# Two chained matmul layers after linear attention: the second stage walks its tokens tile by tile, with x blocks and sums kept in SBUF and weights streamed; the first stage gets its own PSUM pool

## The chip, the cores and the metric

The kernel runs on one core of one Trainium2 chip. The metric is the device time of one execution in microseconds (us). Every time below is of the kernel before the change, from its timed runs or from one profiled execution.

## The reference

```python
kv = einsum('bhsd,bhse->bhde', k, v)          # 8 batches, 8 heads, 576 positions, head_dim 64
o = einsum('bhsd,bhde->bhse', q, kv)
x = o / sqrt(mean(o*o) + 1e-6) * g_norm       # then 4608 tokens x 512
h = x @ w_in;  x = (relu(h)**2) @ w_out       # layer 0: 512 -> 2048 -> 512
h = x @ w_in2; return (h*cos(h)) @ w_out2     # layer 1: 512 -> 2048 -> 512
```

All data is float32; the weights come as float64 and are turned to float32 on the chip.

## The kernel before

Every matmul operand is split into a high part and the rest (names that end in h and l), and a product is three matmuls: high by high, high by low, low by high. This keeps nearly float32 accuracy.

**Stage one** makes the attention output x and, in 72 chunks (9 tiles of 512 tokens by 8 of the 16 groups of 128 hidden columns), the plain product of half of layer 0: `layer_in` (L362) multiplies x by w_in, `act_relu2` squares, `layer_out` (L397) multiplies by w_out and adds up in four accumulators, which `evict` writes to DRAM as `p_d`. x itself goes to DRAM as `x_d`. Beside it the weights of the rest are converted: `conv_w` loads 512 KB of raw words, makes float32 of them on VectorE and ScalarE, and writes the result to DRAM as `wi_d` and `wo_d`.

**Stage two** does the other half of layer 0 (m=0) and all of layer 1 (m=1). The tokens are cut into tiles of 1024 (the fifth has 512), the hidden columns into groups q of 512: two groups for m=0, four for m=1. One tile with one group is a slot; there are 30. A slot's first product uses a scheme with seven block products instead of eight: `x_block` makes seven combinations of the four quadrants of x (each 128 partitions x 1024 numbers, or 512 in a half tile), `first_product` (L480, 12 matmuls each, 84 in a slot) multiplies them by seven combined weight blocks `wi`, into the PSUM tiles FA and FB in turn; `keep`, `add` and `last` take the sums out. Then relu squared, or a chain of seven steps for x*cos(x), gives g, split into gh and gl. The second product (L589, 96 matmuls in a full slot) multiplies g by `wo` into the PSUM tiles SA and SB, and `drain` adds the result to a partial sum.

The order of slots is the order of the loops: group outside, tile inside. So the five tiles pass once for each group, in six rounds, and

```python
slots = [(m, t, q) for m in range(2) for q in groups_of[m] for t in range(len(TILES))]
```

makes slots 0 to 4 the first round, 5 to 9 the second and so on. A round loads its weights once (`if t == 0`). The x blocks are made in the first round of a layer, written to DRAM as `xb_d`, and loaded again for each slot of the layer's other rounds. The partial sums go through DRAM as well: `load_ev` loads 128 x 512 numbers ahead of each unit of 12 matmuls, `drain` (L601 for m=0, L606 for m=1) adds on VectorE and stores.

All loads and stores named here are issued by SyncE (SP), in one order, each when its own waits are over. Jobs have a place in time (`at(pos(slot), ...)`), and the 84 and 96 matmuls of a slot are mixed at a fixed rate. From this the framework makes each engine's order. A PSUM tile of the kernel before holds two banks (`psum[n]` of shape 128 x 2 x 512), in stage one too, where `at_bank` gives each use half of such a tile. While stage two runs, until slot 9, the 16 weight pieces of layer 1 are converted (`pairs_in(1, ...)`).

Of the kernel before, what the change touches and what calls it, by code (L numbers as in the profile page):

```python
# [22 lines left out]
def kernel(  # L23
# [42 lines left out]
    ps_p = ctx.enter_context(tc.tile_pool(name="ps", bufs=1, space=PSUM))  # L66
# [10 lines left out]
    y_d = [dram.tile([P, NKC, 2 * ht], F32, name=f"y_d{t0}") for t0, ht in TILES]  # L77
    o_d = [dram.tile([P, NKC, 2 * ht], F32, name=f"o_d{t0}") for t0, ht in TILES]
    xb_d = {
        (m, t, i): dram.tile([P, 2, 2, ht], F32, name=f"xb_d{m}_{t}_{i}")  # L80
        for m in range(2)
        for t, (t0, ht) in enumerate(TILES)
        for i in range(NPR)
    }
# [11 lines left out]
    psum = {n: ps_p.tile([P, 2, 512], F32, name=n) for n in ("FA", "FB", "SA", "SB")}  # L96
    at_bank = {
        "l0": ("FA", 0), "l1": ("FA", 1), "o": ("FB", 0), "ss": ("FB", 1),
        "acc0": ("SA", 0), "acc1": ("SA", 1), "acc2": ("SB", 0), "acc3": ("SB", 1),
    }  # L100
    banks = {"o": ["o", "acc0", "acc2"], "ss": ["ss", "acc1", "acc3"], "l": ["l0", "l1"]}

    def bank_of(tag):
        n, j = at_bank[tag]
        return psum[n][:, j, :]

    def bank(use):
        tag = banks[use].pop(0)
        banks[use].append(tag)
        return bank_of(tag)  # L110
# [3 lines left out]

    pools = {}
# [274 lines left out]
    def layer_out(t, f):  # L390
        wh, wl = (x[:, 1, :] for x in wts[0, f])
        gh, gl = gs.pop((t, f))
        for i in range(NKC):
            o = bank_of(f"acc{i}")
# [13 lines left out]
    xb, wi, wo, kept, hs, ys, evs2, quads = {}, {}, {}, {}, {}, {}, {}, {}  # L408
# [4 lines left out]
    def load_quads(m, t):  # L413
        t0, ht = TILES[t]
        for a in range(2):
            for s in range(2):
                quads[m, t, a, s] = raw = big("x", F32, "xraw", ht)
                if m == 0:
                    for b, s0, done, n in pieces(t0 + s * ht, ht, S):
                        nc.sync.dma_start(  # L420
                            out=raw[:, :, done:done + n], in_=x_d[b][:, 2 * a:2 * a + 2, s0:s0 + n]
                        )
                else:
                    nc.sync.dma_start(out=raw, in_=y_d[t][:, 2 * a:2 * a + 2, s * ht:(s + 1) * ht])

    def x_block(k, i):
        m, t, q = slots[k]
        ht = TILES[t][1]
        h, l = xb[k, i] = [big("x", F32R, f"x{n}", ht) for n in "hl"]
        if q:  # L430
            for a, x in enumerate((h, l)):
                nc.sync.dma_start(out=as32(x), in_=xb_d[m, t, i][:, a])
            return
        b11, b12, b21, b22 = (quads[m, t, a, s] for a in range(2) for s in range(2))

        def combine(x, y):
            new = big("x", F32, "xt", ht)
            nc.vector.tensor_tensor(out=new, in0=x, in1=y, op=ALU.subtract)
            return new

        if i == 3:
            quads[m, t, "t1"] = combine(b12, b11)
            quads[m, t, "t2"] = combine(b22, quads[m, t, "t1"])
# [3 lines left out]
            2: lambda: quads[m, t, "t1"],  # L447
            3: lambda: quads[m, t, "t2"],
            4: lambda: b22,
            5: lambda: combine(b22, b12),  # L450
            6: lambda: combine(b21, quads[m, t, "t2"]),
# [6 lines left out]
    def load_wi(m, q, i):  # L458
        wi[m, q, i] = w = w_p.tile([P, 2, 2, 2, P], F32R, tag="w", name="wi")
        nc.sync.dma_start(out=as32(w[:]), in_=wi_d[m, q][:, W_OF[i]])  # L460

    def load_wo(m, q, c):
        wo[m, q, c] = w = w_p.tile([P, 2, DM], F32R, tag="w", name="wo")
# [6 lines left out]
    def first_product(k, i):  # L470
        m, t, q = slots[k]
        ps = f_bank(k, i)
        w, x = wi[m, q, i], xb[k, i]
# [76 lines left out]

    def units(k):
# [4 lines left out]
    def load_ev(k, j, i):  # L556
        m, t, q = slots[k]
        t0, ht = TILES[t]
        evs2[k, j, i] = e = temp([P, 512], F32, "ev")
        if m:  # L560
            r = j * (ht // P) + i
            if q:
                nc.sync.dma_start(out=e, in_=o_d[t].rearrange("p c n -> p (c n)")[:, r * DM:(r + 1) * DM])
        elif q:
            nc.sync.dma_start(out=e[:, :ht], in_=y_d[t][:, i, j * ht:(j + 1) * ht])
        else:
            for b, s0, done, n in pieces(t0 + j * ht, ht, TOK):
                nc.sync.dma_start(out=e[:, done:done + n], in_=p_d[b][:, i, s0:s0 + n])

    s_count = [0]  # L570

    def second_unit(k, j, i):
        m, t, q = slots[k]
        ht = TILES[t][1]
        ps = bank_of(f"acc{s_count[0] % 4}")
        s_count[0] += 1
        if m == 0:
            ps = ps[:, :ht]
        cs = slice(i * P, (i + 1) * P)
        n = 0  # L580
        for pp in range(2):
            for u in range(2):
                w, g = wo[m, q, 2 * pp + u], gs[k, (u, j)]
                for a, b in ((0, 0), (0, 1), (1, 0)):
                    if m == 0:
                        lhs, rhs = w[:, a, cs], g[b][:, pp, :]
                    else:
                        lhs, rhs = g[b][:, pp, cs], w[:, a, :]
                    nc.tensor.matmul(ps, lhs, rhs, start=(n == 0), stop=(n == 11), skip_group_check=True)  # L589
                    n += 1  # L590
                    if n == 12:
                        drain(k, j, i, ps)
                    yield

    def drain(k, j, i, ps):
        m, t, q = slots[k]
        t0, ht = TILES[t]
        e = evs2.pop((k, j, i))
        if m == 0:
            e = e[:, :ht]  # L600
            nc.vector.tensor_tensor(out=e, in0=ps, in1=e, op=ALU.add)  # L601
            nc.sync.dma_start(out=y_d[t][:, i, j * ht:(j + 1) * ht], in_=e)
            return
        r = j * (ht // P) + i
        if q:
            nc.vector.tensor_tensor(out=e, in0=ps, in1=e, op=ALU.add)  # L606
        elif i % 2:
            nc.scalar.copy(out=e, in_=ps)
        else:
            nc.vector.tensor_copy(out=e, in_=ps)  # L610
        if q == groups_of[1][-1]:
            nc.sync.dma_start(out=out[t0 + r * P:t0 + (r + 1) * P, :], in_=e)
        else:
            nc.sync.dma_start(out=o_d[t].rearrange("p c n -> p (c n)")[:, r * DM:(r + 1) * DM], in_=e)
# [5 lines left out]
    LAG2 = 1.18  # L620
# [223 lines left out]
```

## Time and profile before

| | |
|---|---|
| three timed runs | 1767.85, 1768.12, 1775.46 us |
| the profiled execution | 1766.62 us, span 1764.8 us |
| granted TensorE clock, mean of the span | 0.984 of full speed |
| TensorE matmul busy | 1666.6 us (94%), 7928 matmuls |
| VectorE (DVE), ScalarE (ACT) busy | 1085.8 us (62%), 943.2 us (53%) |
| moved by DMA | 479.63 MB, 272 GB/s over the span |

The span runs from the first to the last instruction; the profiled time is 1.8 us more. Busy time of matmuls overlaps from one to the next, so a stretch can be slow at a high busy share: the number of matmuls in a stretch says more.

### The profile page before, as it was taken

Reading aid. Unit: us, or ns where it says so; the run is one execution under the profiler, and the core shown is the slowest. Engines: PE = TensorE matmul, PEld = TensorE weight load, DVE = VectorE, ACT = ScalarE, POOL = GpSimd, SP = SyncE. Lnnn points to the kernel's source line nnn. Section 1 sums busy time; section 2 is a strip of 40 time slices with the busy share of each in tenths; the row PEclk is TensorE's granted clock in tenths of the full one; section 3 lists DMA queues with packets and bytes.
Section 4 is the critical chain, followed back from the end, with each engine's and each line's share of the span. In section 5 each row is a group of like instructions: output and inputs, shape, how many; then the busy total and the mean of one; then the engine's idle time right before and its main releaser. Section 6 shows DMA issues by size and latency. Waiting matters only on the chain.

```text
span 1764.8 us, 22062 instructions
## 1 busy us (share of the span) xinstructions
PE 1666.6 (94%) x7928; PEld 1318.5 (75%) x7928; DVE 1085.8 (62%) x1522; ACT 943.2 (53%) x1348; POOL 82.0 (5%) x74
## 2 busy tenths in 40 slices
PE   5899999999999998688889999999999999999998
PEld 3677677767787876566667787888888788887887
DVE  6765777776765676544454677855556555556554
ACT  4766776774435555333343656756445555445542
POOL 0101212221000000000000000000000000000000
PEclk9999999999999998988999999999999999999999
DMA  7555777655478989989998997899988999799863
GB/s 273 187 169 159 249 228 229 181 169 167 140 257 318 351 321 316 288 292 321 297 319 288 379 335 299 318 311 327 321 291 277 336 323 312 251 339 326 297 204 101
DMA packets 252492, 479.63 MB, mean 272 GB/s; under 512 B 23520, under 2 KB 124384, under 8 KB 252384
## 3 DMA queue, kind: packets, MB, share of 16 engines
q1 hardware_dynamic: 251616, 475.88, 79.4%
q0 software_dynamic: 768, 2.36, 0.3%
q8 instruction: 62, 1.02, 0.2%
q14 instruction: 46, 0.38, 0.1%
HBM read 301.99 MB, written 176.16 MB: 271 GB/s over the span
## 4 chain that ended last, share of the span: by engine, by line
PE 71%; DVE 9%; DMA 8%; ACT 7%; issue 3%; SPq 1%; POOL 0%; DVEq 0%; ACTq 0%; POOLq 0%
PE SA L589 14%; PE SB L589 14%; PE FA L480 12%; PE FB L480 11%; PE FA L362 8%; PE SA L397 4%; PE SB L397 4%; PE FB L362 2%; DMA xl<-xb_d 1%; DMA wi_d<-raw 1%; DMA xraw<-x_d 1%; DMA xh<-xb_d 1%; DMA ev<-p_d 1%; PE FB L241 1%; DVE h L504 1%
## 5 line engine op out<-in xcount | busy, mean ns | idle before, releaser
L480 PE MATMUL FB<-xh,wi 128*128 128x512 f32 (+1 forms) x840 | 289.7, 376 | 18.4 <-DMA xh<-xb_d 13.6
L480 PE MATMUL FA<-xh,wi 128*128 128x512 f32 (+1 forms) x840 | 285.5, 372 | 8.0 <-DMA xh<-xb_d 6.2
L589 PE MATMUL SB<-wo,gh 128*128 128x512 f32 x576 | 210.9, 397 | 1.1 <-DVE ev L606 1.1
L589 PE MATMUL SA<-wo,gh 128*128 128x512 f32 x576 | 208.6, 394 | 0.6 <-ACT gh L545 0.6
L480 PEld LDWEIGHTS FB<-xh,wi 128*128 128x128 f32 x840 | 159.6, 192 | 50.8 <-DMA xh<-xb_d 11.2
L480 PEld LDWEIGHTS FA<-xh,wi 128*128 128x128 f32 x840 | 156.9, 189 | 40.1 <-DMA xh<-xb_d 5.9
L521 ACT ACTIVATE y<-h,zerob 128x1024 int32<-128x1024 f32 (+1 forms) x80 | 85.2, 1065 | 173.0 <-DVE h L500 172.5
L480 PE MATMUL FB<-xl,wi 128*128 128x512 f32 (+1 forms) x420 | 158.1, 376 | 4.0 <-DMA xl<-xb_d 3.9
L480 PE MATMUL FA<-xl,wi 128*128 128x512 f32 (+1 forms) x420 | 156.2, 372 | 5.2 <-DMA xl<-xb_d 5.2
L589 PEld LDWEIGHTS SB<-wo,gh 128*128 128x128 f32 x576 | 107.5, 188 | 30.9 <-DVE ev L606 7.7
L589 PEld LDWEIGHTS SA<-wo,gh 128*128 128x128 f32 x576 | 107.5, 188 | 28.4 <-DVE ev L606 3.8
L539 DVE SCALAR_TENSOR_TENSOR y<-y,h 128x1024 f32<-128x1024 f32 (+1 forms) x80 | 89.2, 1115 | 53.4 <-ACT y L535 53.2
L525 DVE SCALAR_TENSOR_TENSOR y<-y,h 128x1024 f32<-128x1024 int32 (+1 forms) x80 | 89.4, 1117 | 53.1 <-ACT y L521 52.2
L589 PE MATMUL SA<-gh,wo 128*128 128x512 f32 (+1 forms) x320 | 109.1, 390 | 10.3 <-DVE ev L601 7.2
L589 PE MATMUL SB<-gh,wo 128*128 128x512 f32 (+1 forms) x320 | 107.3, 382 | 11.6 <-DVE ev L601 11.6
L589 PE MATMUL SA<-wo,gl 128*128 128x512 f32 x288 | 112.8, 392 | 0.2 <-DVE gl L549 0.2
L589 PE MATMUL SB<-wo,gl 128*128 128x512 f32 x288 | 112.7, 391 | 0.0
L549 DVE TENSOR_TENSOR gl<-y,gh 128x1024 fp32r<-128x1024 f32 (+1 forms) x80 | 89.1, 1114 | 33.0 <-ACT gh L545 33.0
L362 PE MATMUL FA<-xh,wh 128*128 128x512 f32 x240 | 98.1, 409 | 5.9 <-ACT xh L331 3.7
L531 ACT ACTIVATE y<-y 128x1024 f32<-128x1024 f32 (+1 forms) x80 | 78.0, 975 | 47.7 <-DVE y L525 47.4
L362 PE MATMUL FA<-xl,wh 128*128 128x512 f32 x240 | 96.0, 400 | 0.1
L362 PE MATMUL FA<-xh,wl 128*128 128x512 f32 x240 | 95.7, 399 | 0.0
(162 smaller groups left out, 3301.0 us busy)
## 6 DMA issues: line engine op xcount, KB each, us to landing
xh<-xb_d SPq DMA_DIRECT2D x112, 512.0 KB, 6.9
xl<-xb_d SPq DMA_DIRECT2D x112, 512.0 KB, 7.1
xb_d<-xh SPq DMA_DIRECT2D x56, 512.0 KB, 5.8
xb_d<-xl SPq DMA_DIRECT2D x56, 512.0 KB, 5.6
o_d<-ev SPq DMA_DIRECT2D x108, 256.0 KB, 4.6
ev<-o_d SPq DMA_DIRECT2D x108, 256.0 KB, 5.0
wi<-wi_d SPq DMA_DIRECT2D x42, 512.0 KB, 6.4
kvld<-in_kv SPq DMA_DIRECT2D x32, 512.0 KB, 7.0
```

What stands on the lines that cost most here:

```text
L241: nc.tensor.matmul(kv_ps[b][r, p, r], t[:n, 0, head], t[:n, 1, head], start=(c == 0 and p == 0), stop=(c == NSC - 1), skip_group_check=True,)
L362: nc.tensor.matmul(ps, a[:, 0, cs], m[:], start=(c == 0 and k == 0), stop=(c == NKC - 1 and k == 2))
L397: nc.tensor.matmul(o, a[:, cs], m[:], start=(f == 0 and n == 0), stop=(f == NH - 1 and n == 2), skip_group_check=True)
L480: nc.tensor.matmul(ps[:, pp, :], a, b, start=(i in (0, 1, 2) and n == 0), stop=(n == 5), skip_group_check=True)
L504: nc.vector.tensor_tensor(out=h, in0=f_bank(k, i), in1=t, op=ALU.add)
L521: nc.scalar.activation(out=y.bitcast(I32), in_=hs[k, b], func=AF.Identity, bias=zerob)
L525: nc.vector.scalar_tensor_tensor(out=y, in0=y.bitcast(I32), scalar=-1.0, in1=hs[k, b], op0=ALU.mult, op1=ALU.add)
L531: nc.scalar.activation(out=y, in_=y, func=AF.Sin, scale=math.pi)
L539: nc.vector.scalar_tensor_tensor(out=y, in0=y, scalar=-2.0 * math.pi, in1=hs.pop((k, b)), op0=ALU.add, op1=ALU.mult)
L549: nc.vector.tensor_tensor(out=l, in0=ys.pop((k, b)), in1=as32(h), op=ALU.subtract)
L589: nc.tensor.matmul(ps, lhs, rhs, start=(n == 0), stop=(n == 11), skip_group_check=True)
```

## The change

- The slots go tile by tile: `(m, t, q)` with q inside. A tile's x blocks are made once and stay in SBUF for its two or four slots; nothing is written to or read from `xb_d`.
- The weights `wi` (seven loads of 512 KB) and `wo` (four) are loaded for every slot.
- The partial sums stay in SBUF: four tiles of 128 x 1024 for a tile's life (`sums`), filled from `p_d` for m=0, stored once at the last group.
- The second product takes four units at a time: it goes through the four `wo` pieces outside and the four units inside, so that four accumulators (two in SA, two in SB) are open together, and `drain` takes two of them in one VectorE instruction of 128 x 1024.
- Stage one has a PSUM pool of its own with eight tiles of one bank; the pool of FA, FB, SA, SB opens after it. A pad of 24 numbers per partition ahead of the stage-one tiles becomes 56.
- The jobs get other places: x quadrants 3.6 products ahead, `wi` 2.7, the conversions of layer 1 from slot 0.5 to 8.4 (before 2.5 to 9.2).

```diff
-    psum = {n: ps_p.tile([P, 2, 512], F32, name=n) for n in ("FA", "FB", "SA", "SB")}
+    pools = {}
+    psum = {}
+    def bank_tile(tag):
+        return pools["ps"].tile([P, 512], F32, tag=tag, name=tag)
...
-    slots = [(m, t, q) for m in range(2) for q in groups_of[m] for t in range(len(TILES))]
+    slots = [(m, t, q) for m in range(2) for t in range(len(TILES)) for q in groups_of[m]]
...
     def x_block(k, i):
...
-        h, l = xb[k, i] = [big("x", F32R, f"x{n}", ht) for n in "hl"]
-        if q:
-            for a, x in enumerate((h, l)):
-                nc.sync.dma_start(out=as32(x), in_=xb_d[m, t, i][:, a])
-            return
...
+        l = src.bitcast(F32R) if i in (0, 4) else big("c" if i == 6 else "x", F32R, "xl", ht)
+        xb[m, t, i] = h, l
         nc.scalar.copy(out=h, in_=src)
         nc.vector.tensor_tensor(out=l, in0=src, in1=as32(h), op=ALU.subtract)
-        for a, x in enumerate((h, l)):
-            nc.sync.dma_start(out=xb_d[m, t, i][:, a], in_=as32(x))
...
+    CHUNKS = (1, 3, 0, 2)
+    def sum_tile(k, n):
+        m, t, q = slots[k]
+        j, i = units(k)[2 * n]
+        t0, ht = TILES[t]
+        if q == 0:
+            sums[m, t, n] = e = w_p.tile([P, 2, 512], F32, tag="w", name="sum")
+            if m == 0:
+                for b, s0, done, size in pieces(t0 + j * ht, ht, TOK):
+                    nc.sync.dma_start(out=e[:, :, done:done + size], in_=p_d[b][:, i:i + 2, s0:s0 + size])
+    def second(k, n):
+        m, t, q = slots[k]
+        ht = TILES[t][1]
+        todo = units(k)[4 * n:4 * n + 4]
+        for a, c in enumerate(CHUNKS):
+            pp, u = divmod(c, 2)
+            w = wo[k, c]
+            for b, (j, i) in enumerate(todo):
+                ps = psum["SA" if b < 2 else "SB"][:, b % 2, :512 if m else ht]
+                g = gs[k, (u, j)]
...
+                    last = a == 3 and (x, y) == (1, 0)
+                    nc.tensor.matmul(
+                        ps, lhs, rhs, start=(a == 0 and (x, y) == (0, 0)), stop=last, skip_group_check=True
+                    )
+                    if last and b % 2:
+                        drain(k, 2 * n + b // 2)
+                    yield
     def drain(k, n):
...
+        if q or m == 0:
+            nc.vector.tensor_tensor(out=e, in0=ps, in1=e, op=ALU.add)
         else:
+            nc.scalar.copy(out=e, in_=ps)
+        if q < groups_of[m][-1]:
+            return
...
-    LAG2 = 1.18
+    LAG2 = 1.12
...
-        (pairs_in(1, range(2 * NP)), pos(2.5), pos(9.2)),
+        (pairs_in(1, range(2 * NP)), pos(0.5), pos(8.4)),
...
+            at(pos(k + (f - 2.7) * PH) if k or f > 2 else nA0 - 5 + f / 2, load_wi, k, i)
+        for a, c in enumerate(CHUNKS):
+            at(pos(k + LAG2 - 0.4 + a / 8), load_wo, k, c)
...
-        right("pad", 1).tile([P, 24], F32, name="pad")
+        right("pad", 1).tile([P, 56], F32, name="pad")
...
-    pools["c"] = ctx.enter_context(tc.tile_pool(name="c", bufs=16, side="left"))
-    pools["t"] = ctx.enter_context(tc.tile_pool(name="t", bufs=8, side="left"))
+    ps_p = ctx.enter_context(tc.tile_pool(name="ps", bufs=1, space=PSUM))
+    psum.update({n: ps_p.tile([P, 2, 512], F32, name=n) for n in ("FA", "FB", "SA", "SB")})
+    pools["c"] = ctx.enter_context(tc.tile_pool(name="c", bufs=18, side="left"))
+    pools["t"] = ctx.enter_context(tc.tile_pool(name="t", bufs=4, side="left"))
```

How the instructions stand on two engines shows what moved. On SP before, in the second round (xh and xl are x blocks, ev a partial sum, wh and raw two parts of a converted weight, raw<-in_wB the load of the next one's words):

```order
L432 DMA xl<-xb_d_1_4_112 128x1024
L565 DMA ev<-y_d_91 128x512
L147 DMA raw<-in_wB 128x2x256 x2
L602 DMA y_d_91<-ev 128x512
L432 DMA xh<-xb_d_1_6_114 128x1024
L432 DMA xl<-xb_d_1_6_114 128x1024
L565 DMA ev<-y_d_91 128x512
L602 DMA y_d_91<-ev 128x512
```

On SP now, in a slot of m=0 at the change of a tile:

```order
L451 DMA wo<-wo_d_8_99 128x1024
L446 DMA wi<-wi_d_1_94 128x1024
L134 DMA raw<-in_wB 128x2x256 x2
L451 DMA wo<-wo_d_10_101 128x1024
L553 DMA sum<-p_d_86 128x1024
L446 DMA wi<-wi_d_1_94 128x1024 x2
L594 DMA y_d_90<-sum 128x1024
L161 DMA wi_d_3_98<-wh 896x1x128
L161 DMA wi_d_3_98<-raw 896x1x128
```

Weights stand where the x blocks stood, the loads and stores of partial sums are fewer and larger, and the conversions' loads and stores are still between them.

On TensorE before, where one unit of the second product ends in SA and the next starts in SA's other bank (a new unit begins with wo_11831):

```order
L589 MATMUL SA_203<-wo_11854,gh_12220 128x512
L480 MATMUL FB_202<-xl_12287,wi_11600 128x512
L480 MATMUL FB_202<-xh_12286,wi_11600 128x512 x2
L480 MATMUL FB_202<-xl_12287,wi_11600 128x512
L589 MATMUL SA_203<-wo_11831,gh_12009 128x512
L589 MATMUL SA_203<-wo_11831,gl_12010 128x512
```

On TensorE now, where the last matmul into SA (the first row) ends a group of four units and the next group starts in SA (wo_11423); four rows of SB and three of FB lie in the cut:

```order
L572 MATMUL SA_5631<-wo_11530,gh_11522 128x512
L467 MATMUL FA_5629<-xl_10745,wi_11512 128x512
L572 MATMUL SB_5632<-wo_11530,gh_11522 128x512
L467 MATMUL FA_5629<-xh_10744,wi_11512 128x512
...
L467 MATMUL FB_5630<-xh_10783,wi_11554 128x512
L572 MATMUL SB_5632<-wo_11530,gh_11522 128x512
L467 MATMUL FB_5630<-xl_10785,wi_11554 128x512
L572 MATMUL SA_5631<-wo_11423,gh_11563 128x512
```

Before, the next matmul into the same PSUM tile is the fifth after the last one of the unit; now it is the 14th at this place, and the 13th or 14th at the others.

## Rows read from the trace of the kernel before

**Rows 1.** Windows of the whole core: length, busy us (count) by engine, granted clock, DMA.

```profile
core 0: us, PE busy (x) PEld busy (x) DVE busy (x) ACT busy (x) POOL busy (x), PEclk, DMA share, GB/s
0.00:544.70 544.70, 510.23 (x2714) 378.59 (x2715) 374.60 (x681) 327.48 (x681) 82.02 (x74) 1.00 0.63 204
544.70:749.80 205.10, 182.72 (x811) 148.11 (x809) 134.52 (x175) 106.41 (x119) 0.00 (x0) 0.96 0.91 319
749.80:983.80 234.00, 204.89 (x889) 162.53 (x890) 109.30 (x176) 86.71 (x94) 0.00 (x0) 0.94 0.91 309
983.80:1180.60 196.80, 190.33 (x897) 157.46 (x896) 147.33 (x151) 130.25 (x147) 0.00 (x0) 0.98 0.88 323
1180.60:1368.10 187.50, 187.34 (x854) 153.35 (x852) 103.10 (x108) 97.44 (x104) 0.00 (x0) 1.00 0.90 306
...
1743.10:1764.80 21.70, 16.32 (x68) 12.07 (x66) 6.73 (x10) 3.71 (x6) 0.00 (x0) 1.00 0.21 80
```

**Rows 2.** The same stretches, L589 (second product) alone.

```profile
544.70:749.80 205.10, 114.31 (x384) 72.94 (x384) 0.96 0.91 319
749.80:983.80 234.00, 125.20 (x468) 86.68 (x468) 0.94 0.91 309
983.80:1180.60 196.80, 132.58 (x475) 85.29 (x475) 0.98 0.88 323
1180.60:1368.10 187.50, 143.85 (x433) 79.35 (x432) 1.00 0.90 306
```

**Rows 3.** The chain that ended last, 690 to 1000 us: start, length, what.

```profile
714.33 6.23 DMA ev<-p_d
...
744.09 6.90 DMA xl<-xb_d
...
767.09 4.21 DMA wi_d<-raw
774.37 7.70 DMA xl<-xb_d
```

**Rows 4.** Waits: engine, line, releaser; us in total, times, longest us.

```profile
DVE ev L601 <- DMA ev<-p_d: 25.1, 6, 13.6
...
PE FB L480 <- DMA xh<-xb_d: 13.6, 6, 8.9
...
PEld SB L589 <- DVE ev L606: 7.7, 21, 1.2
...
PE FA L362 <- ACT og L283: 2.1, 4, 0.8
...
PE FB L299 <- ACT og L283: 1.0, 2, 0.7
```

**Rows 5.** DMA issues: what, count, KB each, median us from issue to landing.

```profile
xh<-xb_d SPq DMA_DIRECT2D x112, 512.0 KB, 6.9
...
xb_d<-xh SPq DMA_DIRECT2D x56, 512.0 KB, 5.8
...
o_d<-ev SPq DMA_DIRECT2D x108, 256.0 KB, 4.6
...
wi<-wi_d SPq DMA_DIRECT2D x42, 512.0 KB, 6.4
...
wo<-wo_d SPq DMA_DIRECT2D x24, 512.0 KB, 7.0
...
raw<-in_wB SPq DMA_DIRECT2D x32, 256.0 KB, 4.1
```

**Rows 6.** Groups of VectorE by shape: count, busy us, mean ns, idle before.

```profile
L606 DVE TENSOR_TENSOR ev<-SB,ev 128x512 f32<-128x512 f32 x54 | 37.3, 690 | 82.0 <-PE SB L589 72.6 <-DMA out<-ev 4.7 <-DMA ev<-o_d 3.5
...
L504 DVE TENSOR_TENSOR h<-FB,m 128x1024 f32<-128x1024 f32 x8 | 9.8, 1224 | 12.7 <-PE FB L480 12.3 <-ACT m L494 0.4
```

**Rows 7.** Timeline at 1405 us: the end of a unit and its drain.

```profile
1405.54 0.39 PE L589 MATMUL SB<-wo,gh 128*128 128x512 f32 x1
...
1405.97 0.69 DVE L606 TENSOR_TENSOR ev<-SB,ev 128x512 f32<-128x512 f32 x1 [0.22 <-PE SB L589]
```

**Rows 8.** The chain that ended last: twelve matmuls in a row in either stage.

```profile
479.03 2.78 PE FA L362 x12
...
1347.49 2.73 PE SA L589 x12
```

More of the change, by code (lines that the diff above doesn't have):

```diff
@@ L76 @@
     p_d = [dram.tile([P, NKC, TOK], F32, name=f"p_d{t}") for t in range(NTILE)]
[L77 to L84, printed above, removed]
+    y_d = [dram.tile([P, 2, NKC, ht], F32, name=f"y_d{t0}") for t0, ht in TILES]
     first_pair = (NP, 0)
@@ L407, with load_quads @@
     BLOCKS = {(0, 0): 2, (1, 1): 5, (0, 1): 6, (1, 0): 7}
-    xb, wi, wo, kept, hs, ys, evs2, quads = {}, {}, {}, {}, {}, {}, {}, {}
+    xb, wi, wo, kept, hs, ys, sums, quads = {}, {}, {}, {}, {}, {}, {}, {}
     def big(pool, dtype, name, ht):
         return pools[pool].tile([P, 2, 512], dtype, tag=pool, name=name)[:, :, :ht]
-    def load_quads(m, t):
+    def load_quads(m, t, a):
         t0, ht = TILES[t]
[L415 to L424, printed above, removed]
+        for s in range(2):
+            quads[m, t, a, s] = raw = big("x", F32, "xraw", ht)
+            if m == 0:
+                for b, s0, done, n in pieces(t0 + s * ht, ht, S):
+                    nc.sync.dma_start(
+                        out=raw[:, :, done:done + n], in_=x_d[b][:, 2 * a:2 * a + 2, s0:s0 + n]
+                    )
+            else:
+                nc.sync.dma_start(out=raw, in_=y_d[t][:, s, 2 * a:2 * a + 2, :])
     def x_block(k, i):
@@ L557, in load_ev, with drain @@
+    def drain(k, n):
         m, t, q = slots[k]
         t0, ht = TILES[t]
[L559 to L565, printed above, removed]
-        else:
-            for b, s0, done, n in pieces(t0 + j * ht, ht, TOK):
-                nc.sync.dma_start(out=e[:, done:done + n], in_=p_d[b][:, i, s0:s0 + n])
@@ L570 @@
[L570 to L576, printed above, removed]
-        if m == 0:
[L578 to L608, printed above, removed]
-        else:
[L610 to L614, printed above, removed]
+        j, i = units(k)[2 * n]
@@ new lines, in drain @@
+        ps = psum[("SA", "SB")[n % 2]]
+        e = sums[m, t, n]
+        if m == 0:
+            e, ps = e[:, :, :ht], ps[:, :, :ht]
+        if q or m == 0:
+            nc.vector.tensor_tensor(out=e, in0=ps, in1=e, op=ALU.add)
+        else:
+            nc.scalar.copy(out=e, in_=ps)
+        if q < groups_of[m][-1]:
+            return
+        if m == 0:
+            nc.sync.dma_start(out=y_d[t][:, j, i:i + 2, :], in_=e)
+        else:
+            r = t0 + j * ht + i * P
+            nc.sync.dma_start(out=out[r:r + 2 * P, :].rearrange("(a p) d -> p a d", p=P), in_=e)
@@ L712 @@
                 at(pos(k + (f + 0.25 * (a + 1)) * PH), fn, k, b)
-        todo = units(k)
-        for n, u in enumerate(todo):
-            at(pos(k + LAG2 + (n - 1.5) / len(todo)), load_ev, k, *u)
+        for n in range(len(units(k)) // 2):
+            at(pos(k + LAG2 - 0.2 + 2 * n / len(units(k))), sum_tile, k, n)
     jobs.sort(key=lambda j: j[:2])
@@ L742, in run_slots @@
         seconds = [
-            (k + LAG2 + (n + a / 12) / len(units(k)), k, u, a)
+            (k + LAG2 + n / len(units(k)) / 12, k, n)
             for k in range(len(slots))
-            for n, u in enumerate(units(k))
-            for a in range(12)
+            for n in range(12 * len(units(k)))
         ]
@@ L749, in run_slots @@
         steps1 = (x for k, i in firsts for x in first_product(k, i))
-        steps2 = (x for s0, k, u, a in seconds if a == 0 for x in second_unit(k, *u))
+        steps2 = (x for s0, k, n in seconds if n % 48 == 0 for x in second(k, n // 48))
         nf, ns = 12 * len(firsts), 0
```

71 lines of the change are left out of this document (36 added, 35 removed).

## The prediction

> **What bounds the kernel now.** I read the windows first, cut where the first product of slots 0, 5, 10, 15 and 20 begins, so that each window is one round of five slots [rows 1]. What is to be seen is the number of matmuls beside the length. Stage one ends at 544.7 us and is nearly all TensorE: 510.2 us busy. The fourth round is what stage two can be: 187.5 us, 187.3 of them busy, clock 1.00. The second round has 889 matmuls, only 35 more, and takes 234.0 us at a clock of 0.94. The first takes 205.1 us for 811.
>
> To compare rounds I make the matmuls equal. Each round has 420 of the first product, 84 of them on the half tile's 256 columns; I count those as half (an estimate: by columns), which leaves 378. The second product adds 433 in the fourth round [rows 2], all of 512 columns, as layer 1 moves the weights: 811 in 187.5 us, 0.231 us each. In rounds two and three 96 of the second product's matmuls are half ones (the half slot of m=0): 378 + 468 - 48 = 798 and 378 + 475 - 48 = 805; round one has 378 + 384 = 762. At 0.231 us they should take 184.5, 186.1 and 176.2 us. They took 234.0, 196.8 and 205.1. So 49.5 + 10.7 + 28.9 = 89 us are lost in rounds one to three, and the fourth is the pace without that loss, at a DMA share of 0.90, hardly below the 0.91 of the slow rounds. The share of the transfers alone is therefore not the reason; what counts is who waits for them.
>
> The chain of waits through the slow stretch goes from transfer to transfer: a partial sum (6.2 us), an x block (6.9), a weight store (4.2), an x block (7.7) [rows 3]. In the table of waits TensorE waits for x blocks, 13.6 us in six waits up to 8.9, and VectorE stands at its drain for partial sums, 25.1 us in six waits up to 13.6 [rows 4]; while it stands, what is queued behind it, the adds that free FA and FB, stands too. Both transfers exist only because x blocks and sums live in DRAM.
>
> **The change part by part.** *Removed.* Of full tiles, 112 loads each of xh and xl and 56 stores each at 512 KB (0.524 MB) are 176 MB, and the sums 108 stores and about as many loads of o_d at 0.262 MB, 57 MB [rows 5]; with the half tiles and y_d (not shown) some 274 MB by my count. *Added.* wi goes from 42 loads to 210, wo from 24 to 120 (seven and four for each of 30 slots): 264 more of 0.524 MB, 138 MB. The total falls from 480 to about 344 MB. A slot of m=0 then moves 5.8 MB of weights, half of three transfers of 2.1 MB (x, p_d, y_d), and two conversions of 1.4 MB: 11.8 MB in 41 us, 288 GB/s. That is less than the 306 GB/s of round four, which costs TensorE nothing [rows 1].
>
> What matters more is the lead. In the list of instructions of the program before, the ten closest loads of xh stand 1 to 14 matmuls ahead of their first use, at most 3.2 us, where one takes 6.9 us to land [rows 5]. In the changed list every wi load stands at least 57 matmuls ahead of its use (13 us) and every wo load 77; they take 6.4 and 7.0 us. The cover is thus twice the price; if it is gone, a product waits for the rest of its load. I take the 89 us as gained, with 40 as the lower end (below, second rival).
>
> *The hand-over of SA and SB.* Now a drain reads 128 x 1024 numbers, and TensorE's next matmul into that tile must wait for it. From the start of the last matmul of a unit to the start of its drain on an idle VectorE it is 0.43 us [rows 7]; an add of that size from PSUM takes 1.22 us [rows 6], together 1.65. The order gives 13 steps of 0.231, 3.0 us. The slack of 1.35 us is one VectorE instruction. Before, a drain of 0.69 us [rows 6] had five steps, 1.16 us for 1.12, and the waits that this made are there: 21 of 0.37 us for weight loads into SB [rows 4], within round four's price. There are 112 such hand-overs (four in each of 26 slots, two in the four half slots of layer 1). If VectorE is always two instructions behind, each costs 2 x 1.22 - 1.35 = 1.1 us, 123 us; if it is on time, none, and the old short waits go too. Since the drains before mostly found VectorE idle (the row of L606 shows it waiting 72.6 us for SB [rows 6]), I take near the lower end: 5 us.
>
> *Conversions.* They run from slot 0.5 on instead of 2.5. In the changed list, VectorE's first instruction on a raw tile stands 11 to 17 matmuls behind its load (before, 65 and more): 2.5 to 3.9 us, against 4.1 us to land [rows 5] and up to 7 if it fares like the other loads. VectorE is then held 0 to 4.5 us, 15 times, and with it drains and adds; the quadrants of x have a like lead at the nine changes of a tile, as before. TensorE feels what exceeds the 1.35 us of slack: 0 to 3.1 us x 24 = 0 to 75 us. Most raw loads should be late by 1 us or so; I take 0.4 us each, 10 us.
>
> *Stage one.* Two things can help. With two uses in one PSUM tile a matmul waits for readers of the other half: the `ss` matmul L299 waits for the read of `o` by L283, 1.0 us, and L362 2.1 us [rows 4]. With other such waits I take 5 us (0 to 10). And twelve matmuls in a row take 2.78 us in stage one, 2.73 in stage two [rows 8]: 0.004 us each, over 1728 matmuls 7 us. Whether the pad's 128 bytes decide that, no row tells; I take half, 4 us (0 to 7). The order of stage one is shuffled as well, which can cost as much as these give.
>
> *The end.* After the last first product 21.7 us remain now [rows 1]. 67 matmuls at 0.231 are 15.5 of them, the rest, 6.2, is drain and store. I leave it.
>
> **The sum.** 1766.6 (the profiled execution) - 89 + 5 + 10 - 9 = 1684 us (rounded). The same from the front: stage one 536, all 2520 + 2688 matmuls of stage two at 0.231 with half ones halved (4860) 1123, new waits 15, end 6, and 2 outside the span: 1682. The profiled execution lies 0.1% under the median of the runs, 1768.1, so I put no correction on it. A change under 0.5% (9 us) is about what a measurement of this kernel cannot tell from none.
>
> **The rivals.**
>
> *VectorE held by loads.* The 24 holds above cost 2 us each instead of 0.4: 38 us more, 1722. For it speaks that VectorE's standing at a drain is already what most of the lost time goes through [rows 4]; against it, that the x quadrants had the same short lead in the first round, which lost less than the second, where none are loaded.
>
> *Weights late: slower.* SP issues in order, and between the weights stand the conversions' stores, which wait for VectorE and ScalarE. If SP is held for longer than the lead of 13 us less 6.4, each product starts late. The loss is at most in the first nine slots, where the conversions are, 63 products. From (89 + 9 - 15) / 63 = 1.3 us per product it takes back the whole gain; at 1.6 us, a quarter of a load, the time is 1785. Against it speaks only the lead; no row tests a stream of weights. If half of the loss of rounds one and two stays in this way, the time is 1684 + 39 = 1723, the same as the first rival.
>
> *The conversions were the cause.* The chain of waits holds weight stores too [rows 3]. If the slow rounds are slow because of them, the loss of rounds one and two stays, 78 us: 1762, no change.
>
> *The clock.* In round four TensorE pauses for drains and the clock stays 1.00 [rows 1, 4]. If closer hand-overs in all of stage two brought the 0.94 of round two, its 1123 us would be 1195: 1756. The Trainium skill (TensorE: Matmul & The Clock Gate, A second HAM failure mode: psum-queue depth-cycling) speaks of a kernel whose cycling through PSUM in each iteration makes TensorE pause often enough to lower its clock again and again. By that rule this rival would come true; round four, with its short pauses, does not bear it out.
>
> *Everything hidden.* No new waits and both gains of stage one in full: 1684 - 15 - 8 = 1661.
>
> **How the numbers follow.** Forecast, 1665 to 1705: 0.60. One of the two half-way cases, 1705 to 1745: 0.17. Everything hidden or better, under 1665: 0.11. Conversions or clock, 1750 to 1770: 0.05. Weights or hand-overs that cost more than was gained, over 1776: 0.07. The range for 8 in 10 is 1661 to 1730; it leaves out half of the lowest case, a third of the half-way cases and the two last. Faster than 1759: 0.60 + 0.17 + 0.11 and a little of the clock's case, 0.89; within 0.5%: 0.04; slower: 0.07.
>
> **What would show it.** Right: windows of five slots' worth of work in slots 0 to 9 at the pace of the fourth round, clock 1.00 from 560 us on, about 344 MB moved, no TensorE wait for a DMA over 2 us in stage two, waits of TensorE for drains below 10 us in all. The first rival would show as VectorE waits for raw and xraw of some 50 us with TensorE waiting behind L588; late weights as TensorE waits for wi; the clock's case as a clock under 0.97 without long waits. Wrong would be the whole argument if slots 0 to 9 took over 45 us each although no x block is loaded.

## The result and the profile after

The changed kernel takes 1623.28 us (median of four runs, 1620.51 to 1626.28); the kernel before, beside it, 1770.49. The ratio is 0.9166, 95% interval 0.9137 to 0.9195. The forecast was 1684 us with a range from 1661: the direction was right, the gain is 147 us where 84 were forecast, and the time lies 38 us below the range.

The windows of the whole core, cut at the end of stage one and at slots 5, 10, 15 and 20 (columns as in [rows 1]; the slots of a window are others than before, as the tiles now lie outside):

```profile
0.00:497.55 497.55, 476.62 (x2721) 376.10 (x2721) 377.00 (x700) 324.61 (x684) 81.30 (x74) 1.00 0.66 215
497.55:679.89 182.34, 180.54 (x793) 148.67 (x794) 125.75 (x166) 104.66 (x108) 0.00 (x0) 1.00 0.88 296
679.89:865.22 185.33, 180.91 (x901) 152.29 (x900) 108.37 (x135) 87.75 (x102) 0.00 (x0) 0.99 0.82 277
865.22:1058.30 193.08, 193.08 (x903) 161.61 (x901) 118.06 (x104) 114.64 (x114) 0.00 (x0) 1.00 0.56 187
1058.30:1262.30 204.00, 204.00 (x902) 168.89 (x901) 118.64 (x101) 116.96 (x113) 0.00 (x0) 1.00 0.49 163
...
1603.86:1621.60 17.74, 12.65 (x57) 9.85 (x55) 8.06 (x10) 4.38 (x8) 0.00 (x0) 0.93 0.16 60
```

Two things are to be seen. Stage one ends at 497.55 us instead of 544.70 [rows 1], 47 us earlier. And in slots 15 to 19, five full ones, TensorE is busy all of 204.00 us: 40.80 us per slot of 180 matmuls, 0.2267 us each, at a clock of 1.00.

What TensorE waits for in stage two now (columns as in [rows 4]):

```profile
PE SA L572 <- ACT wh L157: 2.7, 2, 2.2
PE SA L572 <- DVE sum L588: 2.3, 2, 1.7
PE FA L467 <- issue: 1.3, 1, 1.3
PE SB L572 <- DVE sum L588: 1.1, 2, 0.6
```

No transfer is among them, where [rows 3, 4] had x blocks and partial sums. The drains cost 3.4 us in four waits of matmuls; in the rows of the weight loads (PEld), which stand apart, they are 5.1 us, also in four. The new streams of weights land in time, and the bytes are those that were counted (columns as in [rows 5]; the last line is the page's total):

```profile
wi<-wi_d SPq DMA_DIRECT2D x210, 512.0 KB, 4.6
wo<-wo_d SPq DMA_DIRECT2D x120, 512.0 KB, 4.6
...
DMA packets 169572, 344.27 MB, mean 212 GB/s; under 512 B 15360, under 2 KB 92672, under 8 KB 169472
```

The drain of 128 x 1024 numbers takes what was priced, and mostly waits for TensorE, not the other way round (groups of VectorE by shape, as [rows 6]):

```profile
L588 DVE TENSOR_TENSOR sum<-SA,sum 128x1024 f32<-128x1024 f32 x43 | 52.5, 1221 | 30.2 <-PE SA L572 30.1
L588 DVE TENSOR_TENSOR sum<-SB,sum 128x1024 f32<-128x1024 f32 x43 | 52.4, 1219 | 12.1 <-PE SB L572 12.0
...
L116 DVE TENSOR_SCALAR e<-raw 128x512 uint32<-128x512 uint32 x15 | 6.4, 426 | 39.6 <-DMA raw<-in_wB 39.5
```

The last row is the hold of VectorE by raw tiles (the loaded words of a weight, ahead of its conversion) that the forecast feared: 39.5 us, in 11 waits.

### The profile page after: what moved, and what is told of

The parts are those of the page before. It is cut to its first block, busy times and chain, and to the rows that moved or that the text cites. A ratio compares the mean times of both kernels' runs of the same rounds, so it can differ in the third digit from the quotient of the medians.

```text
span 1621.6 us, 21070 instructions
## 1 busy us (share of the span) xinstructions
PE 1589.4 (98%) x7928; PEld 1305.7 (81%) x7928; DVE 1056.2 (65%) x1410; ACT 947.9 (58%) x1348; POOL 81.3 (5%) x74
## 2 busy tenths in 40 slices
DMA packets 169572, 344.27 MB, mean 212 GB/s; under 512 B 15360, under 2 KB 92672, under 8 KB 169472
## 4 chain that ended last, share of the span: by engine, by line
PE 88%; DMA 5%; DVE 4%; ACT 2%; issue 1%; SPq 1%; POOL 0%; DVEq 0%; POOLq 0%
PE SB L572 17%; PE SA L572 17%; PE FA L467 15%; PE FB L467 15%; PE acc L386 10%; PE l L349 9%; DMA wi_d<-raw 1%; PE o L349 1%; DMA xraw<-x_d 1%; DMA wi<-wi_d 1%; PE ss L349 1%; DMA q<-in_qT 1%; DVE sum L588 1%; PE l L228 0%; PE o L262 0%
## 5 line engine op out<-in xcount | busy, mean ns | idle before, releaser
L467 PE MATMUL FA<-xh,wi 128*128 128x512 f32 (+1 forms) x840 | 304.0, 368 | 1.4 <-issue 1.3
L467 PE MATMUL FB<-xh,wi 128*128 128x512 f32 (+1 forms) x840 | 304.0, 368 | 0.0
L572 PE MATMUL SA<-wo,gh 128*128 128x512 f32 x576 | 223.1, 390 | 0.0
L526 DVE SCALAR_TENSOR_TENSOR y<-y,h 128x1024 f32<-128x1024 f32 (+1 forms) x80 | 89.4, 1117 | 95.8 <-ACT y L522 95.8
L572 PE MATMUL SA<-gh,wo 128*128 128x512 f32 (+1 forms) x320 | 118.2, 372 | 5.0 <-ACT wh L157 2.7
L386 PE MATMUL acc<-gh,wh 128*128 128x512 f32 x288 | 113.6, 396 | 0.0
L386 PE MATMUL acc<-gl,wh 128*128 128x512 f32 x288 | 112.9, 392 | 0.0
L386 PE MATMUL acc<-gh,wl 128*128 128x512 f32 x288 | 112.6, 391 | 0.0
L572 PE MATMUL SB<-gh,wo 128*128 128x512 f32 (+1 forms) x320 | 111.5, 370 | 1.1 <-DVE sum L588 1.1
L467 PE MATMUL FA<-xl,wi 128*128 128x512 f32 (+1 forms) x300 | 110.5, 368 | 0.0
L467 PE MATMUL FB<-xl,wi 128*128 128x512 f32 (+1 forms) x300 | 110.3, 368 | 0.0
```

What stands on the lines that cost most here:

```text
L386: nc.tensor.matmul(o, a[:, cs], m[:], start=(f == 0 and n == 0), stop=(f == NH - 1 and n == 2), skip_group_check=True)
L467: nc.tensor.matmul(ps[:, pp, :], a, b, start=(i in (0, 1, 2) and n == 0), stop=(n == 5), skip_group_check=True)
L526: nc.vector.scalar_tensor_tensor(out=y, in0=y, scalar=-2.0 * math.pi, in1=hs.pop((k, b)), op0=ALU.add, op1=ALU.mult)
L572: nc.tensor.matmul(ps, lhs, rhs, start=(a == 0 and (x, y) == (0, 0)), stop=last, skip_group_check=True)
```

## The experiments

Each run was timed beside the kernel before on the same chip, where that took 1766.6 to 1767.8 us (medians); a ratio is to that median. The changed kernel's 1623.28 us were measured on another occasion, beside 1770.49, so a difference of a few us to it is uncertain by about as much as those two differ from each other, 3 us.

### Stage one: the pad and the PSUM tiles, each alone and each undone

```diff
-        right("pad", 1).tile([P, 24], F32, name="pad")
+        right("pad", 1).tile([P, 56], F32, name="pad")
```

The kernel before with the pad alone.

> The kernel before with the pad of 56 alone: the same instructions in the same order on every engine, only the right-hand tiles of stage one move by 128 bytes. Theory A (most of the 47 us that stage one gained comes from PSUM tiles of one bank, the pad gives only the shorter step of a matmul): twelve matmuls of stage one go from 2.78 to about 2.73 us, 1728 x 4.4 ns = 8 us, so 1770.5 - 8 = 1762 us, stage one ends at about 537 us. Theory B (the place of the tiles in memory is behind most of it): stage one ends at about 505 us, 1730 us. Theory C (the place decides nothing): 1770 us, step unchanged.

Measured: 1761.34 us, ratio 0.9966 (0.9950 to 0.9981); stage one ends at 539.4 us.

```diff
+        return pools["ps"].tile([P, 512], F32, tag=tag, name=tag)
...
-            o = bank_of(f"acc{i}")
+            if f == 0:
+                accs[i] = bank_tile(f"acc{i}")
+            o = accs[i]
```

The kernel before with the PSUM pool of one-bank tiles in stage one, the pad left at 24.

> The kernel before with a PSUM pool of stage one of its own, eight tiles of one bank, pad 24 as before. Theory A: stage one loses its waits for the other half of a tile, 35 to 40 us; it ends at about 507 us, the time is 1730 to 1736 us; the step of a matmul in stage one stays at 0.232 us. Theory B: at most 10 us, 1760 us or more.

Measured: 1732.27 us, ratio 0.9777 (0.9742 to 0.9812); stage one ends at 503.4 us. The order of TensorE's instructions in stage one is that of the changed kernel.

The changed kernel with the pad of 24 again.

> The changed kernel with the pad of 24 again: the order of TensorE's instructions is the same. Theory A: +8 us, 1631 us, stage one ends at about 506 us with a step of 0.232 us. Theory B: stage one ends at 535 us or more, 1660 us. Theory C: no change, 1623 us.

Measured: 1630.52 us, ratio 0.9222 (0.9208 to 0.9235), 7.2 us over the changed kernel; stage one ends at 503.7 us.

The changed kernel with `at_bank` and the four tiles of two banks in stage one again.

> The changed kernel with the four PSUM tiles of two banks in stage one again, pad 56. Theory A: stage one ends at about 537 us, 1623 + 39 = 1662 us. Theory B: at most 10 us more, 1633 us. In both the pace of stage two, 40.8 us for a full slot, stays.

Measured: 1665.91 us, ratio 0.9424 (0.9410 to 0.9439), 42.6 us over; stage one ends at 538.0 us, and the full slots of stage two stay at 40.8 us.

So theory A holds from both sides: the tiles, with the order of instructions that comes with them, give 36 to 43 us, the pad 6 to 7 (by the ratios, up to 10). Where the tiles' part was before is in the waits of the weight loads (PEld), which I had not added up. First the kernel before, up to the end of stage one:

```profile
PEld FB L241 <- DMA kvld<-in_kv: 12.1, 5, 9.3
PEld FA L362 <- ACT og L283: 4.8, 9, 1.2
...
PEld FB L299 <- DVE m L312: 3.6, 6, 1.0
PEld FB L299 <- ACT og L283: 3.4, 6, 1.2
PEld SB L271 <- DVE m L312: 3.0, 1, 3.0
```

and the same view with one-bank tiles, same pad:

```profile
PEld o L235 <- DMA kvld<-in_kv: 12.1, 5, 9.3
...
PEld ss L293 <- DVE m L306: 2.9, 5, 1.7
PEld acc L291 <- ACT sq L276: 2.5, 2, 2.0
PEld ss L291 <- ACT sq L276: 2.3, 1, 2.3
```

`og` (L283) reads the attention output `o`, which lay in one half of FA or FB; L362 and L299 write the other half. Those two rows are gone, and the wait of `ss` for its own last reader, `m`, stays. Over all rows of this view that name a releaser, the sum falls from 66.9 to 31.1 us: 36 us, about what the time fell by. With the pad alone it is 67.9, with the two-bank tiles put back into the changed kernel 68.2. The rest of the difference between the lists is many rows under 3 us. The two sums agree; that each of these waits cost its full length is not shown, as a weight load can wait while matmuls still run.

The effect is also seen where busy time shows nothing. L362 alone in the stretches 88 to 352 and 352 to 497 us, before:

```profile
88.00:352.00 264.00, 109.29 (x431) 79.12 (x432) 1.00 0.65 203
352.00:497.00 145.00, 71.16 (x286) 52.82 (x285) 1.00 0.50 157
```

and the same product with one-bank tiles:

```profile
88.00:352.00 264.00, 118.60 (x472) 86.43 (x472) 1.00 0.66 212
352.00:497.00 145.00, 76.04 (x310) 58.03 (x308) 1.00 0.61 206
```

TensorE was busy 260.5 of the 264 us before, and yet the kernel with one-bank tiles has 472 of these matmuls in the same stretch instead of 431, a tenth more.

The pad shows in the step. Twelve matmuls in a row in the chain that ended last, with the pad alone:

```profile
400.87 2.72 PE FA L362 x12
```

and with one-bank tiles and the pad of 24:

```profile
402.19 2.79 PE o L356 x12
```

The median step of a matmul of 512 columns in stage one is 232 ns in the kernel before and the two of these runs with the pad of 24, and 227 ns in the changed kernel and the two with 56; stage two has 227 in all six.

### The pace of stage two

```diff
-        ps = bank_of(f"acc{s_count[0] % 4}")
+        ps = psum[f"acc{s_count[0] % 4}"][:]
...
+    psum.update({f"acc{i}": ps2.tile([P, 512], F32, name=f"acc{i}") for i in range(4)})
```

The kernel before with SA and SB cut into one-bank tiles in stage two only.

> The kernel before with the second product of stage two in four PSUM tiles of one bank in place of SA and SB; stage one and all transfers as before. Theory (a drain of one half of a tile holds TensorE's next matmul into the other half, 0.57 us in each slot): where nothing else is waited for, a full slot goes from 41.37 to about 40.8 us; some 20 such slots, -11 us, 1757 us. Rival (the drain is late on VectorE whatever the tile is): 41.4 us, 1768 us.

Measured: 1750.35 us, ratio 0.9908 (0.9883 to 0.9933): 16 us, where 11 were expected. Windows of two full slots without conversions:

```profile
1246.00:1286.80 40.80, 40.80 (x182) 33.80 (x181) 23.07 (x23) 21.21 (x21) 0.00 (x0) 1.00 0.96 336
1286.80:1327.60 40.80, 40.80 (x182) 33.80 (x181) 23.08 (x23) 21.21 (x21) 0.00 (x0) 1.00 0.82 273
```

In the kernel before such a slot takes 41.37 us:

```profile
1252.91:1294.28 41.37, 41.37 (x181) 33.55 (x180) 23.16 (x24) 20.97 (x21) 0.00 (x0) 1.00 0.93 317
```

The 0.57 us per slot are the waits of [rows 4] for the drain of the other half (7.7 us in 21 waits for SB). The changed kernel takes the drains of both halves in one, and gets the same 40.80.

### x blocks, sums and conversions

```diff
-        (pairs_in(1, range(2 * NP)), pos(2.5), pos(9.2)),
...
-        nc.sync.dma_start(out=as32(w[:]), in_=wi_d[m, q][:, W_OF[i]])
+        nc.sync.dma_start(out=as32(w[:]), in_=wi_d[0, q % 2][:, W_OF[i]])
```

The kernel before without layer 1's conversions.

> The kernel before without the 16 conversions of layer 1's first weights (layer 1 reads those of layer 0, so the output is another one); x blocks and sums go through DRAM as before. Theory 1 (the trips of x blocks and sums through DRAM cost the 89 us by themselves): the rounds one and two keep 60 us or more of their loss, 1750 us or more. Theory 2 (the trips cost only where conversions load the queues, VectorE and ScalarE, the loss begins at 660 us, where the first conversion stands): slots 2 to 11 run at 41.4 us, 1680 to 1690 us.

Measured: 1687.12 us, ratio 0.9542 (0.9513 to 0.9572): theory 2. The stretch from 693.74 to 897.61 us, before and then without conversions:

```profile
693.74:897.61 203.87, 165.20 (x720) 131.86 (x718) 100.39 (x171) 74.12 (x86) 0.00 (x0) 0.90 0.92 307
```

```profile
693.74:897.61 203.87, 202.46 (x979) 168.08 (x978) 69.47 (x85) 77.60 (x83) 0.00 (x0) 1.00 0.94 328
```

979 matmuls instead of 720, at a DMA share that is even higher. x blocks and sums go through DRAM in both, so without conversions these trips cost next to nothing in this order: the full slots of the second round take 41.4 us, the pace of the rounds without loss.

```diff
+        h, l = xb[k, i] = [big("x", F32R, f"x{n}", ht) for n in "hl"]
+        if q:
+            for a, x in enumerate((h, l)):
+                nc.sync.dma_start(out=as32(x), in_=xb_d[m, t, i][:, a])
+            return
```

The changed kernel with the x blocks through DRAM. The edit also takes back how the blocks are made: the quadrants are loaded all at once, each block gets new buffers, and in the slot that makes them they stand 1.5 products ahead instead of 1.9. So this run and the two others with it measure the trip and this together.

> The changed kernel, tile by tile, but with x blocks stored and loaded again for each later group of a tile, at the leads of the kernel before; sums stay in SBUF. Theory (the trip of the x blocks makes most of the 89 us, where conversions run): slots 1, 3, 5, 7, 9 lose 5 us or more each, 1650 to 1680 us. Rival (the sums, or the order of tiles and groups, make most): 1635 us or less.

Measured: 1756.61 us, ratio 0.9943 (0.9920 to 0.9965): 133 us more than the changed kernel, beyond what the theory gave. TensorE's waits in its stage two:

```profile
PE SA L582 <- DMA wo<-wo_d: 30.8, 13, 5.2
PE FB L477 <- DMA xh<-xb_d: 10.2, 5, 6.5
PE SB L582 <- ACT sum L600: 9.9, 8, 1.2
PE FB L477 <- DVE w L124: 7.5, 1, 7.5
```

```diff
+        if q and m:
+            nc.sync.dma_start(out=e, in_=o_d[t][:, n])
+        elif q:
+            nc.sync.dma_start(out=e[:, :, :ht], in_=y_d[t][:, j, i:i + 2, :])
...
+        if m and q < groups_of[m][-1]:
+            nc.sync.dma_start(out=o_d[t][:, n], in_=e)
```

The changed kernel with the sums through DRAM.

> The changed kernel with the sums stored and loaded again at each later group, x blocks kept. Theory as for the run with x blocks: VectorE's 25.1 us at drains before came from sums, so 1640 to 1655 us if the sums are a good part. Rival (x blocks alone): within 5 us of 1623. Both runs together over 1623 by some 80 us would account for the whole gain of rounds one to three; much less would leave the order of tiles as a part of its own.

Measured: 1622.62 us, ratio 0.9182 (0.9158 to 0.9205). It moves 419.81 MB instead of 344.27 and costs nothing. This is in the changed order and beside x blocks that are kept; the sums beside x blocks that go through DRAM were not tried apart.

Two more runs complete the table: the changed kernel without conversions, and with x blocks through DRAM and without conversions.

> The changed kernel without layer 1's 16 conversions (layer 1 reads layer 0's first weights, so the output is another one). All theories: what conversions still cost is gone; 1611 us if they are behind all of the 12 us that slots 0 to 7 lose, 1618 us or more if the making of x blocks has a part.

Measured: 1613.69 us, ratio 0.9133 (0.9120 to 0.9146).

> The changed kernel with x blocks through DRAM and without layer 1's conversions (output another one). Theory C (x blocks through DRAM cost 133 us only together with the conversions): 1625 to 1645 us. Rival D (the bytes of x blocks and streamed weights are too many by themselves): 1700 us or more.

Measured: 1678.18 us, ratio 0.9493 (0.9470 to 0.9516): between the two theories. Some 64 us are there without any conversion, so theory C fails for this kernel, which also streams the weights; its first 162 us of stage two run at 370 GB/s. But in the full slots of layer 0 this loss does not stand where blocks are loaded. Slot 4, which makes and stores its blocks, and slot 5, which loads them (from first product to first product):

```profile
643.24:691.32 48.08, 45.19 (x188) 36.36 (x189) 28.97 (x25) 24.30 (x24) 0.00 (x0) 0.96 0.98 379
691.32:732.00 40.68, 39.48 (x173) 32.02 (x171) 10.09 (x10) 13.57 (x14) 0.00 (x0) 1.00 0.90 353
```

With kept blocks and without conversions both take 40.8 us. In stage two TensorE waits for x loads 0.8 us in all here, and the chain that ended last goes through ScalarE and VectorE, which make the blocks, where slot 4 begins (columns as in [rows 3]):

```profile
642.16 1.05 ACT xh L448
...
644.37 1.22 DVE xl L449
```

So at least a part of the 64 us goes with the making and storing of blocks, and not with the loads. Beside conversions the slots that load are the longest: slots 3 and 5 take 57.0 and 57.1 us in the first run with x blocks through DRAM, 40.7 here.

| | with conversions | without | difference |
|---|---|---|---|
| before (x blocks through DRAM) | 1766.6 | 1687.1 | 79.5 |
| changed, x blocks through DRAM | 1756.6 | 1678.2 | 78.4 |
| changed (x blocks kept) | 1623.3 | 1613.7 | 9.6 |

The conversions cost 79 us beside x blocks that go through DRAM, in either order of slots, and 10 us beside kept ones.

### What the two collide on

In the kernel before, SyncE's own waits between 660 and 1060 us begin with the conversions' stores and loads:

```profile
SPq L174 <- ACT wh L170: 70.0, 15, 7.8
SPq L147 <- DMA wi_d<-raw: 29.1, 13, 4.0
```

The next three runs move these to another queue.

```diff
-                nc.sync.dma_start(out=wi_d[m, q][:, :, k, pp, i, :], in_=as32(x))
+                (nc.gpsimd if m else nc.sync).dma_start(out=wi_d[m, q][:, :, k, pp, i, :], in_=as32(x))
```

(and the loads of raw tiles alike).

> The kernel before with the loads and stores of layer 1's 16 conversions issued by GpSimd's queue, which is empty in stage two, in place of SyncE's; the same bytes at about the same time. Theory Q (SyncE issues in order and stands for each conversion, 70 us in 15 waits for ScalarE's wh and 29 us for the raw tiles, and the loads of x blocks queue behind it): the loss of rounds one and two goes as without conversions, about 1690 us. Theory D (the bytes of conversions and x blocks together are more than the DMA engines move in time): still 1750 us or more. Theory E (VectorE's and ScalarE's time for conversions delays the drains): also 1750 us or more.

Measured: 1707.69 us, ratio 0.9661 (0.9646 to 0.9675). 59 of the 79.5 us go, with the same bytes and the same work on VectorE and ScalarE, and neither row is left among SyncE's waits. What stood behind these two rows comes in time now. TensorE's largest wait for x blocks between 544 and 1060 us, before and then in this run:

```profile
PE FB L480 <- DMA xh<-xb_d: 13.6, 6, 8.9
```

```profile
PE FB L480 <- DMA xh<-xb_d: 2.1, 1, 2.1
```

All its waits for x blocks there fall from 28.9 to 4.1 us, and VectorE's waits for partial sums from 40.5 to 8.5, so in the kernel before the sums were late by the same queue, and their share is not parted from that of the x blocks. The transfers on GpSimd's queue are also cut otherwise, 221261 packets in all instead of 252492; what that does to the time is not parted either.

> The changed kernel with the same move of queue. Theory Q: the 12 us that slots 0 to 7 still lose go in part, 1612 to 1618 us. Theories D and E: 1623 us.

Measured: 1693.53 us, ratio 0.9592 (0.9573 to 0.9611): 70 us slower than the changed kernel. All theories missed it.

> The changed kernel with x blocks through DRAM (as in the earlier run, 1757 us) and the conversions' transfers on GpSimd's queue. Theory Q: 1640 us or less, nearly all of the 133 us go. Theory D: 1740 us or more, since the DMA share there is 0.99 to 1.03 between 660 and 960 us. Between the two: both count.

Measured: 1799.25 us, ratio 1.0181 (1.0165 to 1.0197): slower by 43 us than with SyncE's queue. What differs in the last two is seen on VectorE. Its first instruction on a raw tile, in the changed kernel on GpSimd's queue (columns as above):

```profile
L116 DVE TENSOR_SCALAR e<-raw 128x512 uint32<-128x512 uint32 x15 | 6.4, 426 | 95.8 <-DMA raw<-in_wB 95.8
```

With the x blocks through DRAM the same waits go from 33.0 to 128.4 us. A load of a raw tile stands behind the store that frees its buffer; the queue issues it only when that store has landed, and VectorE, which has come to the next conversion, stands meanwhile, with the drains and the adds behind it. The queues' own waits for that store between 498 and 860 us, in the changed kernel and then on GpSimd's queue:

```profile
SPq L134 <- DMA wi_d<-raw: 29.3, 14, 4.4
```

```profile
POOL raw L134 <- DMA wi_d<-raw: 69.5, 14, 8.4
```

The transfers land later there too: a raw load after 6.1 us instead of 4.1 (medians). 39.5 us of waits on VectorE stand beside a loss of at most 10 us, 95.8 us beside one of some 80. Two runs test it with a third buffer:

```diff
+            if m and (2 * f + i) % 3 == 2:
+                raw = w_p.tile([P, 4, P, 2], U32, tag="w", name="raw")
```

> The changed kernel with every third raw tile of layer 1's conversions in the pool w, so that a load need not wait until the store of the last but one conversion has landed. Theory V (VectorE stands 39.5 us in 11 waits for raw tiles, and this is what the conversions still cost): the waits fall under 10 us and most of the 10 us between 1623 and the 1614 without conversions go, 1614 to 1618 us. Rival (the conversions' own work on VectorE and ScalarE costs it): 1623 us.

Measured: 1617.35 us, ratio 0.9153 (0.9131 to 0.9175); five runs, 1616.64 to 1618.52, all below the four of the changed kernel, though the intervals of the ratios overlap and the two were timed on different occasions. The waits of VectorE fall only to 25.9 us (its row, below), not under 10 as expected, but TensorE no longer waits for `wh`. By the medians 6 of the 10 us are gone; that is not clear of the noise.

```profile
L116 DVE TENSOR_SCALAR e<-raw 128x512 uint32<-128x512 uint32 x15 | 6.4, 424 | 25.9 <-DMA raw<-in_wB 25.9
```

> The changed kernel with the conversions' transfers on GpSimd's queue (1694 us) and the third raw tile. Theory V: VectorE's 95.8 us of waits for raw tiles made the 70 us, since each load stood behind a store, and a third tile breaks that chain only in part, as GpSimd's queue still issues in order: 1625 to 1660 us. Rival (GpSimd's queue itself or its transfers disturb the rest): 1690 us.

Measured: 1666.60 us, ratio 0.9426 (0.9402 to 0.9451). The theory's upper bound is missed by 7 us. VectorE's waits for raw tiles fall from 95.8 to 58.7 us and the time by 27: so much of the 70 us hangs on the buffers. The other 43 us, and what else GpSimd's queue adds, stay open; the length of VectorE's waits alone does not give the loss, since 58.7 us of them stand beside a loss of 53 here.

### The lead of the weights

```diff
-            at(pos(k + (f - 2.7) * PH) if k or f > 2 else nA0 - 5 + f / 2, load_wi, k, i)
+            at(pos(k + (f - 1.7) * PH) if k or f > 2 else nA0 - 5 + f / 2, load_wi, k, i)
```

> The changed kernel with each wi load asked for one product later (1.7 products ahead instead of 2.7), so that its cover falls from 13 to some 7 us, against 4.6 us to land by the median. Theory (the cover is ample): 1623 to 1630 us. Rival (SyncE's waits eat the cover where conversions run): slots 0 to 8 lose more, 1640 us or more.

Measured: 1620.37 us, ratio 0.9170 (0.9147 to 0.9193): no slower. Half the cover is enough.

## Why the prediction was wrong

The direction was right, the size was not, by 61 us. Its second sum (from the front) shows where:

| term | forecast | measured |
|---|---|---|
| stage one ends | 536 | 497.6 |
| 4860 matmuls of stage two | at 0.231: 1123 | at 0.2267: 1102 |
| new waits, half ones over half, end | 15 + 6 | (1621.6 - 497.6) - 1102 = 22 |
| outside the span | 2 | 2.1 |

**Stage one: -9 where it was -47, the step that failed.** "With other such waits I take 5 us (0 to 10)" rests on the matmul rows alone, L299 and L362 in [rows 4]. A wait that a weight load takes is in a row of its own, and these rows sum to 67 us before and 31 with the one-bank tiles, which took 36 us off the kernel before. The upper bound of 10 was no bound from rows. "The order of stage one is shuffled as well, which can cost as much as these give" had no row behind it either; the order came with the tiles, and no run parts the two. The pad's term (4 of 0 to 7) was right in kind: 6 to 7 us.

**The pace: 0.231 where it was 0.2267, 21 us.** The fourth round was taken as the pace without loss. It holds 0.57 us per full slot of waits for the other half of SA or SB, as one-bank tiles there showed. The text says that these short waits lie "within round four's price" and go if the drains are on time, and then keeps that price for the new kernel and adds 5 us to it.

**The 89 us: right in size, wrong in half of the cause.** All of that loss is gone but what the conversions still cost, 10 us. But the sums, which made the largest row of VectorE's waits for transfers [rows 4], cost nothing when they alone are put back into the changed kernel. The rival "the conversions were the cause" is half right: taking out the conversions alone gives 79.5 us; putting the x blocks' trips back, with the way of making that goes with them, costs 133 in the changed order, 64 of them without any conversion. In the order of before the trips cost next to nothing without conversions; conversions without the trips were tried only in the changed order, where they cost 10 us. In the kernel before most of it (59 us) goes when the conversions leave SyncE's queue: it had stood for a conversion, and the x blocks and sums behind it were late. The remaining 20 us, and how the 133 us divide between loads, stores, making and order, are not settled.

**New waits: right in sum, in part by luck.** 15 us were taken for hand-overs and holds; drains cost TensorE 3.4 us, the conversions at most 9.6. The 10 us for holds came from a guess, 24 of them at 0.4 us each. What came were 11 holds of VectorE of 3.6 us on average, 39.5 us in all, of which TensorE lost less than a quarter: the three slots that are longer than without conversions (3, 5 and 7) lose 2.0, 6.0 and 1.5 us. On GpSimd's queue, where the holds are longer, the loss is that of the first rival and more. Late weights did not come, even with half of the cover. The clock: 0.99 to 1.00 in all windows of stage two up to the last, although SA, SB, FA and FB are filled and drained in each slot (the last, where the work runs out, has 0.93). The rule of the Trainium skill (TensorE: Matmul & The Clock Gate, A second HAM failure mode: psum-queue depth-cycling), that such cycling makes the clock fall again and again, is not borne out here: the clock of 0.90 between 693 and 898 us before is 1.00 there without conversions, with the same cycling.

"Everything hidden", 1661, was the lowest case, and it bounded the two small terms by what I had priced. The first was priced from the rows I had found, not from all the waits of stage one, and no row was sought for a full slot without waits.

## What to carry to other kernels

Add up the waits of an engine over all its rows, the weight loads' too, before bounding what a change of buffers can give; a busy share of 98% (88 to 497 us) and the two rows looked at hid 36 us. Where two uses share a PSUM tile, each waited here for the other's readers: give each bank its own tile, or drain both in one instruction. When two streams disturb each other, take out each alone, and both: here the conversions cost 79 us beside x blocks that go through DRAM and 10 us beside kept ones, so neither "x blocks" nor "conversions" alone was the cause. When a run puts an old way back, see what else comes back with it; and before moving a stream to another queue, look at what its loads will then stand behind.

## What the runs showed of the hardware

The same program, the same instructions in the same order, runs its stage-one matmuls of 512 columns in steps of 232 or of 227 ns, depending on 128 bytes in the place of the tiles in SBUF (the kernel before with the pad of 24 and of 56, and the changed kernel with both). With 24 numbers in the pad the tiles of x and g start 128 bytes past a multiple of 256 in a partition, with 56 at a multiple; the tiles that stage two adds start at multiples in all four kernels, and its matmuls have 227 ns. Which of the operands counts, and whether 256 is the step that matters, was not tried.
